# Rows 256 to 511 of x by two crossbar copies of 128 rows, with the early gate in 128-column halves, in a SwiGLU feed-forward kernel

## The chip, the cores and the metric

The kernel runs on one core of a Trainium2 chip. The metric is the device time of one execution in microseconds (us); the time before is the median of 3 runs. The engines named below are PE (TensorE, matrix multiplication; its weight loads are listed as PEld), ScalarE (ACT), VectorE (DVE), GpSimd (POOL) and SP, which here only issues transfers (DMA). A transfer that ScalarE issues stands in a queue of its own. Matmuls write to PSUM, which has few banks; everything else lives in SBUF, the on-chip memory of 128 partitions.

## The reference

```python
B, S, D, F = 1, 2048, 640, 1536          # x: B,S,D  w_gate, w_up: D,F  w_down: F,D, all bfloat16

def reference(x, w_gate, w_up, w_down):
    g = _silu(x @ w_gate)
    u = x @ w_up
    return (g * u) @ w_down
```

## The kernel before

**Tiles.** The 2048 rows of x are worked on in 4 blocks of 512 (`S_BLK`); D is 5 chunks of 128 (`KD`), F is 12 chunks of 128 (`KF`). The gate and up products are computed transposed: for each f chunk, PE multiplies a 128x128 piece of `wg_sb` (or `wu_sb`), loaded as weights, with 512 columns of `xT`, the transposed x, and adds up 5 such products in a PSUM tile `pg` (or `pu`) of 128 x 512. That is `proj` (L195 to L203), and its arguments `c0` and `c1` choose the columns of the block. `gate` (L210 to L217) follows: ScalarE writes silu(pg) to `sg` (L214), VectorE multiplies it with `pu` into `aT` (L215). When all 12 f chunks of a block are done, the down products (L273 and L302) give the block's output rows.

**How x gets transposed.** For the first block, rows 0 to 255 are loaded plainly into `x_sb` (L85, one load from SP's queue and one from ScalarE's), and PE transposes them (`transpose_chunk`, L183 to L193), with copies from PSUM by ScalarE and VectorE. Rows 256 to 511 come by a transposing crossbar copy straight from the HBM into `xT`: `turn_x(PE_X, SUB)` at L121, with `PE_X` = 2 and `SUB` = 4 in units of 128 rows; the copy itself is L109. The other blocks of x come by crossbar copies of 512 rows (L138, L322, L324).

**The order of the transfers.** SP issues in program order: one x load (L85); three loads of the first 512 columns of `w_gate`, kd by kd (L120; ScalarE's queue carries kd 2 and 3); the crossbar copy of rows 256 to 511 (L109); `wu_sb` for f chunks 0 and 1, then for 2 and 3 (L123, L124, issued at L82); the loads of `wg_sb` and `wu_sb` in two pieces of 4 chunks each (L126, L127); `wd_sb` (L128); the crossbar copy of the next 512 rows; `x_row` (L139), and transposing copies of w_gate (`wgT`, L134), which VectorE uses for the last 4 rows. Transfers take completion semaphores in turn from a set of eight, and from the ninth on each waits until the transfer eight places before it has landed.

**The head.** `head` (L219 to L254) sets the order of the first block by hand. PE does 18 warm-up matmuls on a tile of ones (L179), transposes two chunks of x (L188), and then works on the first 4 f chunks (`N_EARLY`): first on columns 0 to 255, kd by kd as the weights land (L240), the very first kd in two halves of 128 columns; then on columns 256 to 511 for each f chunk (L247 and L248, the matmuls being at L197), for which the crossbar copy is needed; then for each f chunk the up product over all 512 columns (L251), followed by `gate`. `keep_order` holds PE, ScalarE, VectorE and SP to the order in which the program states their instructions. The loop over the remaining f chunks (L257 to L267) follows. Its `pg` and `pu` tiles come from the same four PSUM buffers (tag `gu`) as the four early `pg`; the early `pu` use the buffers of the output tiles (`po_a`, `po_b`).

Of the kernel before, what the change touches and what calls it, by code (L numbers as in the profile page):

```python
# [10 lines left out]
def _body(  # L11
# [9 lines left out]
    P = nc.NUM_PARTITIONS  # L21
# [13 lines left out]
    S_BLK = 512  # L35
    NSB = S // S_BLK
    SUB = S_BLK // P
    DA = 512
    Q = 32
    N_WARM, N_EARLY = 18, 4  # L40
    T = 4
    WT_STEP = 4
    PE_X = 2
# [14 lines left out]
    wg_sb = consts.tile([P, KD, F], bf16)  # L58
# [19 lines left out]
    def wslice(a, b):  # L78
        return slice(a * P, b * P)
# [17 lines left out]
    def keep_order(engine):  # L97

        traced = [i for i in nc.cur_bb.bb.instructions if i.engine == engine]
        for a, b in zip(traced, traced[1:]):  # L100
            issue_order(a, b)
# [5 lines left out]
    def turn_x(c0, c1):  # L107
        s_sl = slice(c0 * P, c1 * P)
        nc.sync.dma_start_transpose(out=xT[:, :, s_sl], in_=xt_v[s_sl])  # L109
# [4 lines left out]
    for eng, k0, k1 in (  # L114
# [3 lines left out]
        (nc.sync, 4, 5),  # L118
    ):
        eng.dma_start(out=wg_sb[:, k0:k1, f_sl], in_=wg_v[:, k0:k1, f_sl])  # L120
    turn_x(PE_X, SUB)  # L121
    nc.scalar.activation(silu_first[:], ones[:, 0:1], ACT.Silu)
    load_w(nc.sync, wu_sb, wu_v, 0, N_EARLY // 2)  # L123
    load_w(nc.sync, wu_sb, wu_v, N_EARLY // 2, N_EARLY)  # L124
# [52 lines left out]
    def warm(n):  # L177
        for _ in range(n):
            nc.tensor.matmul(  # L179
                pw[:, 0:P], lhsT=ones[:], rhs=ones[:], start=True, stop=True  # L180
            )

    def transpose_chunk(c, parts):  # L183
        c_sl = slice(c * P, (c + 1) * P)
        for copy, tag, k0, k1 in parts:
            pt = psum.tile([P, k1 - k0, P], bf16, tag=tag, name="pt")
            for kd in range(k0, k1):
                nc.tensor.transpose(  # L188
                    out=pt[:, kd - k0, :],
                    in_=x_sb[:, c, kd * P : (kd + 1) * P],  # L190
                    identity=ident[:],
                )
            copy(out=xT[:, k0:k1, c_sl], in_=pt[:])  # L193

    def proj(ps, w_sb, fc, sb, c0, c1):  # L195
        for kd in range(KD):
            nc.tensor.matmul(  # L197
                ps[:, c0:c1],
                lhsT=w_sb[:, kd, fc * P : (fc + 1) * P],
                rhs=xT[:, kd, sb * S_BLK + c0 : sb * S_BLK + c1],  # L200
                start=(kd == 0),
                stop=(kd == KD - 1),
            )  # L203

    def gu_tiles():
        pg = psum.tile([P, S_BLK], f32, tag="gu", name="pg", bufs=4)
        pu = psum.tile([P, S_BLK], f32, tag="gu", name="pu", bufs=4)
        return pg, pu

    def gate(pg, pu, sb, fc, n_s):  # L210

        s0 = sb * S_BLK
        sg = work.tile([P, S_BLK], f32, name="sg")
        nc.scalar.activation(sg[:, 0:n_s], pg[:, 0:n_s], ACT.Silu)  # L214
        nc.vector.tensor_tensor(  # L215
            out=aT[:, fc, s0 : s0 + n_s], in0=sg[:, 0:n_s], in1=pu[:, 0:n_s], op=ALU.mult
        )  # L217

    def head():  # L219

        dve, act = nc.vector.tensor_copy, nc.scalar.copy
        split = [(act, "po_a", 0, 2), (dve, "po_b", 2, KD)]
        late = PE_X * P
        warm(N_WARM)
        transpose_chunk(0, split)
        transpose_chunk(1, split)  # L230
        pg = [
            psum.tile([P, S_BLK], f32, tag="gu", name="pg", bufs=4)
            for _ in range(N_EARLY)
        ]
        early = [(0, 0, P), (0, P, late)] + [(kd, 0, late) for kd in range(1, KD)]
        for kd, c0, c1 in early:
            for fc in range(N_EARLY):


                nc.tensor.matmul(  # L240
                    pg[fc][:, c0:c1],
                    lhsT=wg_sb[:, kd, wslice(fc, fc + 1)],
                    rhs=xT[:, kd, c0:c1],
                    start=(kd == 0 and c0 == 0),
                    stop=(kd == KD - 1),
                )
        for fc in range(N_EARLY):  # L247
            proj(pg[fc], wg_sb, fc, 0, late, S_BLK)  # L248
        for fc in range(N_EARLY):
            pu = psum.tile([P, S_BLK], f32, tag="po_b" if fc % 2 else "po_a", name="pu")  # L250
            proj(pu, wu_sb, fc, 0, 0, S_BLK)  # L251
            gate(pg[fc], pu, 0, fc, S_BLK)
        keep_order(mybir.EngineType.PE)
        keep_order(mybir.EngineType.Activation)  # L254

    head()
    for sb in range(NSB):  # L257
        n_s = S_BLK if sb < NSB - 1 else S_BLK - T
        for fc in range(KF):
            if sb == 0 and fc < N_EARLY:  # L260
                continue
            pg, pu = gu_tiles()
# [134 lines left out]
def kernel(tc, *args):  # L397
    _body(tc, *args)
    tc.close()
    tc.compile()  # L400
    _trim(tc.nc)
# [30 lines left out]
```

## Time and profile before

| what | value |
|---|---|
| median of 3 runs | 163.23 us (162.78 to 163.5) |
| the profiled execution, its own time | 163.16 us |
| its span, first to last instruction | 161.8 us |
| PE busy | 158.9 us (98%), 796 matmuls |
| weight loads (PEld) busy | 77.1 us (48%) |
| VectorE busy | 110.9 us (69%) |
| ScalarE busy | 42.7 us (26%) |
| chain that ended last | PE 96%, DMA 2%, SP's queue 1% |
| the 20 early gate matmuls on columns 256 to 511 | 272 ns each from start to end, 6.6 to 8.8 us |
| moved by transfers | 15.86 MB, 98 GB/s over the span |

The span lies inside the execution's own time; the difference, 1.36 us, is around it. A matmul's duration goes from its start to the modelled end of its result and so overlaps the next one; the distance from start to start is what counts for a row of them. The chain that ended last is found by going back from the last instruction, at each step to what released it or to the instruction before it on its engine.

### The profile page before, as it was taken

To read this page: it belongs to the slowest core of one execution; us is meant where nothing else is said; L and a number is where in the kernel's file an instruction comes from. 1 tells how busy PE (TensorE), PEld (TensorE's weight loads), DVE (VectorE), ACT (ScalarE), POOL (GpSimd) and SP (SyncE) were. 2 spreads that over 40 slices of the span, in tenths; PEclk is the share of its full clock that TensorE was granted. 3 is DMA by queue.
4 is the path that set the end of the run, shared out by engine and by line. 5 is a ranking of instruction groups with operands and counts; after the bars stand their busy time and mean duration, and the time that the engine had idled before them with its cause. 6 is when DMAs were issued, how large, how long until landed. Compare 5 with 4: busy or idle time off the path is not lost.

```text
span 161.8 us, 2113 instructions
## 1 busy us (share of the span) xinstructions
PE 158.9 (98%) x796; PEld 77.1 (48%) x796; DVE 110.9 (69%) x249; ACT 42.7 (26%) x74; POOL 0.6 (0%) x6
## 2 busy tenths in 40 slices
PE   8999999999999999999999999999999999999995
PEld 7754444444444444444444444444444444445454
DVE  1035223599469999989919999979964999993000
ACT  5131222112222222211222322221214222222121
POOL 1000000000000000000000000000000000000000
DMA  7999999995189991003110000000321000000312
GB/s 226 265 344 350 363 218 231 245 189 101 35 186 166 228 226 39 4 0 34 65 65 0 0 4 2 0 0 4 61 67 34 0 0 0 0 0 4 50 39 73
DMA packets 41801, 15.86 MB, mean 98 GB/s; under 512 B 33216, under 2 KB 41664, under 8 KB 41792
## 3 DMA queue, kind: packets, MB, share of 16 engines
q1 hardware_dynamic: 33296, 14.78, 38.0%
q10 hardware_dynamic: 8496, 0.95, 3.9%
q8 instruction: 6, 0.10, 0.3%
q14 instruction: 3, 0.02, 0.1%
HBM read 6.88 MB, written 2.62 MB: 59 GB/s over the span
## 4 chain that ended last, share of the span: by engine, by line
PE 96%; DMA 2%; SPq 1%; DVE 0%; issue 0%
PE pu L197 32%; PE pg L197 31%; PE po_a L302 26%; PE po_t L273 6%; DMA wg_sb<-in_w_gate_dram 2%; PE pg L240 1%; SPq L120 0%; SPq L85 0%; DVE ot_b L314 0%
## 5 line engine op out<-in xcount | busy, mean ns | idle before, releaser
L197 PE MATMUL pu<-xT,wu_sb 128*128 128x512 bf16 (+1 forms) x240 | 59.0, 379 | 0.0
L197 PE MATMUL pg<-xT,wg_sb 128*128 128x512 bf16 (+2 forms) x240 | 56.9, 370 | 0.0
L215 DVE TENSOR_TENSOR aT<-sg,pu 128x512 bf16<-128x512 f32 (+1 forms) x48 | 32.8, 683 | 32.3 <-PE pu L197 32.3
L214 ACT ACTIVATE sg<-pg 128x512 f32<-128x512 f32 (+1 forms) x48 | 28.5, 596 | 70.7 <-PE pg L197 65.7
L302 PE MATMUL po_a<-wd_sb,aT 128*128 128x512 bf16 (+2 forms) x216 | 42.8, 358 | 0.0
L150 DVE SCALAR_TENSOR_TENSOR prod<-wgT,x_row 128x640 f32<-128x640 bf16 x48 | 39.4, 821 | 1.1
L150 DVE SCALAR_TENSOR_TENSOR prod<-wuT,x_row 128x640 f32<-128x640 bf16 x48 | 39.5, 822 | 1.0
L197 PEld LDWEIGHTS <-wu_sb 128*128 128x128 bf16 x240 | 23.5, 98 | 28.0
L197 PEld LDWEIGHTS <-wg_sb 128*128 128x128 bf16 x240 | 23.5, 98 | 26.1
L302 PEld LDWEIGHTS <-aT 128*128 128x128 bf16 x216 | 20.7, 98 | 21.7
L311 ACT CAST ot<-po_a 128x512 bf16<-128x512 f32 (+1 forms) x17 | 9.5, 560 | 32.0 <-PE po_a L302 20.9
L273 PE MATMUL po_t<-aT,wd_sb 128*128 128x512 bf16 (+1 forms) x48 | 10.4, 366 | 0.0
L273 PEld LDWEIGHTS <-wd_sb 128*128 128x128 bf16 x48 | 4.7, 98 | 5.1
L314 DVE CAST ot_b<-po_a 128x128 bf16<-128x128 f32 x1 | 0.3, 292 | 9.9 <-PE po_a L302 9.9
L282 ACT CAST ot_t<-po_t 128x512 bf16<-128x512 f32 (+1 forms) x4 | 2.2, 558 | 11.6 <-PE po_t L273 11.6
L150 DVE DVE_READ_ACCUMULATOR prod<-wuT,x_row 128x1 f32 x48 | 4.0, 83 | 0.0
L150 DVE DVE_READ_ACCUMULATOR prod<-wgT,x_row 128x1 f32 x48 | 4.0, 82 | 0.0
L284 DVE STREAM_TRANSPOSE ot_q<-ot_t 128x512 bf16<-128x512 bf16 (+1 forms) x4 | 2.7, 678 | 1.7 <-ACT ot_t L282 1.7
L240 PE MATMUL pg<-xT,wg_sb 128*128 128x256 bf16 (+1 forms) x24 | 2.6, 255 | 0.4 <-DMA wg_sb<-in_w_gate_dram 0.4
L193 DVE COPY xT<-pt 128x384 bf16<-128x384 bf16 x2 | 0.7, 358 | 3.2 <-PE pt L188 3.1
L179 PE MATMUL pw<-ones 128*128 128x128 bf16 x18 | 2.1, 313 | 0.4 <-DVE ones L105 0.4
L240 PEld LDWEIGHTS <-wg_sb 128*128 128x128 bf16 x24 | 1.9, 98 | 0.8 <-DMA wg_sb<-in_w_gate_dram 0.7
(15 smaller groups left out, 7.7 us busy)
## 6 DMA issues: line engine op xcount, KB each, us to landing
wd_sb<-in_w_down_dram SPq DMA_DIRECT2D x1, 1920.0 KB, 13.6
out_dram<-ot SPq DMA_DIRECT2D x15, 128.0 KB, 1.7
wg_sb<-in_w_gate_dram SPq DMA_DIRECT2D x2, 640.0 KB, 8.0
wu_sb<-in_w_up_dram SPq DMA_DIRECT2D x2, 640.0 KB, 8.6
wu_sb<-in_w_up_dram SPq DMA_DIRECT2D x2, 320.0 KB, 5.1
x_row<-in_x_dram SPq DMA_DIRECT2D x1, 640.0 KB, 5.0
wg_sb<-in_w_gate_dram SPq DMA_DIRECT2D x3, 128.0 KB, 3.8
out_dram<-ot_q ACTq DMA_DIRECT2D x12, 32.0 KB, 1.9
```

What stands on the lines that cost most here:

```text
L150: nc.vector.scalar_tensor_tensor(out=prod[:], in0=wT[:, fc, :], scalar=1.0, in1=x_row[:, t, :], op0=ALU.mult, op1=ALU.mult, accum_out=acc[ ...
L179: nc.tensor.matmul(pw[:, 0:P], lhsT=ones[:], rhs=ones[:], start=True, stop=True)
L193: copy(out=xT[:, k0:k1, c_sl], in_=pt[:])
L197: nc.tensor.matmul(ps[:, c0:c1], lhsT=w_sb[:, kd, fc * P : (fc + 1) * P], rhs=xT[:, kd, sb * S_BLK + c0 : sb * S_BLK + c1], start=(kd == 0 ...
L214: nc.scalar.activation(sg[:, 0:n_s], pg[:, 0:n_s], ACT.Silu)
L215: nc.vector.tensor_tensor(out=aT[:, fc, s0 : s0 + n_s], in0=sg[:, 0:n_s], in1=pu[:, 0:n_s], op=ALU.mult)
L240: nc.tensor.matmul(pg[fc][:, c0:c1], lhsT=wg_sb[:, kd, wslice(fc, fc + 1)], rhs=xT[:, kd, c0:c1], start=(kd == 0 and c0 == 0), stop=(kd == ...
L273: nc.tensor.matmul(po_t[:], lhsT=wd_sb[:, kf, DA:D], rhs=aT[:, kf, sb * S_BLK : sb * S_BLK + n_t], start=(kf == 0), stop=(kf == KF - 1),)
L282: nc.scalar.copy(ot_t[:], po_t[:])
L284: nc.vector.transpose(out=ot_q[:], in_=ot_t[:])
L302: nc.tensor.matmul(po[:], lhsT=aT[:, kf, s0 : s0 + P], rhs=wd_sb[:, kf, c0:c1], start=(kf == 0), stop=(kf == KF - 1),)
L311: nc.scalar.copy(ot[:], po[:])
```

## The change

The crossbar copy of rows 256 to 511 is issued as two copies of 128 rows, one behind the other on SP. The gate products of the four early f chunks on these rows run in two passes: first columns 256 to 383 for f chunks 0 to 3, then columns 384 to 511 for f chunks 0 to 3. Each pass has 4 x 5 = 20 matmuls of 128 columns, each with its weight load, so that there are 40 in place of 20 of 256 columns. PE's first matmul of the first pass waits for the first copy, its first of the second pass for the second copy. All lines behind the change stand one or two lines lower in the changed kernel; the order of all other instructions on each engine stays the same. The extra transfer shifts the eight semaphores that transfers use in turn by one place.

```diff
@@ -118,7 +118,8 @@
         (nc.sync, 4, 5),
     ):
         eng.dma_start(out=wg_sb[:, k0:k1, f_sl], in_=wg_v[:, k0:k1, f_sl])
-    turn_x(PE_X, SUB)
+    turn_x(PE_X, PE_X + 1)
+    turn_x(PE_X + 1, SUB)
     nc.scalar.activation(silu_first[:], ones[:, 0:1], ACT.Silu)
     load_w(nc.sync, wu_sb, wu_v, 0, N_EARLY // 2)
     load_w(nc.sync, wu_sb, wu_v, N_EARLY // 2, N_EARLY)
@@ -244,8 +245,9 @@
                     start=(kd == 0 and c0 == 0),
                     stop=(kd == KD - 1),
                 )
-        for fc in range(N_EARLY):
-            proj(pg[fc], wg_sb, fc, 0, late, S_BLK)
+        for c0 in range(late, S_BLK, P):
+            for fc in range(N_EARLY):
+                proj(pg[fc], wg_sb, fc, 0, c0, c0 + P)
         for fc in range(N_EARLY):
             pu = psum.tile([P, S_BLK], f32, tag="po_b" if fc % 2 else "po_a", name="pu")
             proj(pu, wu_sb, fc, 0, 0, S_BLK)
```

## The prediction

> **What bounds the kernel now.** I read the chain of waits first: 96% of the span is TensorE (PE), and after one wait for a weight load no other piece comes from anything but PE until the closing eviction.
>
> ```profile
> 0.91 3.89 DMA wg_sb<-in_w_gate_dram
> 4.85 1.92 PE pg L240 x16
> 6.77 2.18 PE pg L197 x20
> 8.95 4.32 PE pu L197 x20
> ```
>
> The columns are start, length, what. The chain starts running without holes at 4.85 us, when the second piece of the gate weights has landed. The PE timeline of the first microseconds says the same, with the idle time and its releaser in brackets:
>
> ```profile
> 3.84 0.64 PE L240 MATMUL pg<-xT,wg_sb 128*128 128x128 bf16 x8
> 4.85 1.92 PE L240 MATMUL pg<-xT,wg_sb 128*128 128x256 bf16 x16 [0.37 <-DMA wg_sb<-in_w_gate_dram]
> 6.61 2.35 PE L197 MATMUL pg<-xT,wg_sb 128*128 128x256 bf16 x20
> 8.79 4.48 PE L197 MATMUL pu<-xT,wu_sb 128*128 128x512 bf16 x20
> 13.11 1.24 PE L197 MATMUL pg<-xT,wg_sb 128*128 128x512 bf16 x5
> ```
>
> The third row is the work that the change cuts up. It has no bracket: PE does not wait for the crossbar copy. How near that is comes from SP's timeline (issue start, issue length) and from the DMA view (last number: us from issue to landing, asked for one issue at a time).
>
> ```profile
> 1.86 1.64 SPq L109 DMA_TRANSPOSE xT<-in_x_dram  x1
> 3.55 1.33 SPq L82 DMA_DIRECT2D wu_sb<-in_w_up_dram  x2
> ...
> 44.56 2.83 SPq L109 DMA_TRANSPOSE xT<-in_x_dram  x1
> ```
>
> ```profile
> xT<-in_x_dram SPq DMA_TRANSPOSE x1, 4.6
> ...
> wu_sb<-in_w_up_dram SPq DMA_DIRECT2D x1, 320.0 KB, 4.8
> ```
>
> The copy lands at 1.86 + 4.6 = 6.46, PE reaches it at 6.61: 0.15 us of slack. The first wu load lands at 3.55 + 4.8 = 8.35; PE loads weights from it at 8.68: 0.33 of slack. The second lands near 4.25 + 5.4 = 9.65 (the pair's median is 5.1, so the other took 5.4) for 8.79 + 10 x 0.216 = 10.95: 1.3. The next wg load (issued 4.93, 6.5 to landing) lands at 11.43 for about 12.9: 1.5; the wu load after it (5.50 + 7.8 = 13.30) is needed at 13.97: 0.67. The tightest loads are thus the copy and the first wu load.
>
> **Part 1, the matmuls.** Removed: 20 matmuls of 256 columns (4 f chunks x 5 kd), 8.79 - 6.61 = 2.18 us, 109 ns each. Added: 40 of 128 columns, with 20 weight loads more. Price of one from two rows of that width, by form:
>
> ```profile
> L302 PE MATMUL po_a<-wd_sb,aT 128*128 128x128 bf16 x12 | 0.8, 219 | 0.0
> L240 PE MATMUL pg<-xT,wg_sb 128*128 128x128 bf16 x8 | 0.6, 220 | 0.0
> ```
>
> Each busy time is (count - 1) spacings plus one duration. At the kernel's end: (0.8 - 0.219)/11 = 0.053 us. At L240, with the timeline's 0.64: (0.64 - 0.220)/7 = 0.060. Both have a new weight load for every matmul, as the new code has. I take 0.0555, between them: 40 x 0.0555 = 2.22, so +0.04; ends -0.06 and +0.22. The far bound is the 18 warm-up matmuls of the same width, (2.10 - 0.313)/17 = 0.105 us apart, which would make +2.0; they run before 2.5 us with durations of 313 ns, and the L240 row, 3 us before the place in question, has 220, so I leave that end to a rival.
>
> The Trainium skill, in "TensorE: Matmul & The Clock Gate", section "Back-to-back issue gap", speaks against the edit: in a stream of weight load and matmul pairs it gives about 81 ns for each of 128 columns, against 56 for one alone. By it the part would be an estimated 40 x 0.081 - 2.18 = +1.1 us, and the time some 164.2. The two rows above show the smaller figure, but in runs of 8 and 12, not 40, and the measured spacing decides for me.
>
> **Part 2, who waits for the gate.** The gate of chunk 0 is complete after 25 of the 40, at 6.61 + 25 x 0.0555 = 8.0 instead of about 7.2, the others 0.28 apart. ScalarE's silus start near 8.2 in place of 7.35 and run 0.6 each, so three are done by 10.0. Their reader is VectorE's product, which waits for pu: 10.14, 11.22, 12.30, 13.38 in the timeline. The fourth silu waits for the first product today (10.87) and still will. Nothing of it reaches PE, whose next use of a gate buffer is at 13.11. Cost 0, cover 1.3 us and more.
>
> **Part 3, the copies' issue on SP.** A copy of 256 rows takes 1.64 us to issue, one of 512 rows 2.83. That is 0.45 fixed and 0.60 per 128 rows; one of 128 takes about 1.05, two 2.1, and everything behind them on SP (all wu, wg and wd loads, the next crossbar copies) is issued 0.45 later. From the ninth transfer on, each DMA of the queue waits for the one eight before it, and the extra copy turns this by one: the first wu load now waits for the x load that lands at 0.12 + 2.9 = 3.0 (SP is there after 3.9), the next wg load for ScalarE's wg load that lands at 0.55 + 4.1 = 4.65 (SP is there at about 5.4). Neither binds. The 0.45 is covered too: the first wu load is issued at 3.55, but the rings still carry the crossbar packets until about 6.05, a cover of 2.5 us. Without that cover the load would land at 8.80 and cost 0.1.
>
> **Part 4, the copies on the rings.** The DMA columns of the table by stretches (the last two: share, GB/s) show what a crossbar copy does there:
>
> ```profile
> 4.50:4.75 0.25, 0.00 (x0) 0.00 (x0) 0.00 (x0) 0.00 (x0) 0.00 (x0) 1.00 1.69 176
> 4.75:5.00 0.25, 0.15 (x2) 0.14 (x3) 0.00 (x0) 0.00 (x0) 0.00 (x0) 1.00 0.36 80
> 5.00:5.25 0.25, 0.25 (x4) 0.23 (x3) 0.00 (x0) 0.00 (x0) 0.00 (x0) 1.00 1.29 287
> ...
> 6.00:6.25 0.25, 0.25 (x5) 0.23 (x3) 0.00 (x0) 0.00 (x0) 0.00 (x0) 1.00 1.09 150
> ...
> 48.75:49.00 0.25, 0.25 (x3) 0.13 (x2) 0.25 (x1) 0.08 (x1) 0.00 (x0) 1.00 0.30 71
> 49.00:49.25 0.25, 0.25 (x3) 0.13 (x2) 0.25 (x1) 0.25 (x1) 0.00 (x0) 1.00 0.43 102
> ```
>
> The bytes and the 256 B packets stay the same; what a second copy can add is a second start. The start at 4.5 to 5.0 loses, against 290 GB/s, (114 + 210) x 0.25 = 81 KB, 0.28 us. Between two crossbar copies behind each other, 48.5 to 50.25, the same count (190, 71, 102, 158, 182, 130, 223 GB/s) loses 243 KB, 0.84 us; but those are limited by their issue of about 3 us for 655 KB, and here the second copy is issued by about 4.0, before the first has run. So the gap is between 0 (loss goes with the rows, not the copies: 0.84 for 512 rows is 0.42 for 256, about what the front copy loses) and 0.84; I take 0.28. Then the first half lands by 6.46 at the latest, for 6.61; the second at 6.74, and PE gets to it after 20 matmuls, 6.61 + 1.11 = 7.72: hidden by 1.0. The first wu load lands at 8.63, wanted at 8.68 + 0.04: hidden by 0.1. With 0.84 it lands at 9.19 and PE stalls 0.47; the later loads have more slack than that, so the stall isn't paid twice.
>
> **The sum.** The profiled execution took 163.16 us, 161.8 of span and 1.36 around it; the median of the three runs is 163.23. Matmuls +0.04, the rest 0: 163.20 on the profiled time, 163.27 on the median. I predict 163.3. What the split opens, gate work before all 256 rows are there, buys nothing, since PE has other work until 6.61 and the copy is there at 6.46.
>
> **The rivals.**
> *A start for each copy.* The gap is 0.84, the first wu load stalls PE at 8.7: 163.2 + 0.47 = 163.7. For it: the low stretch after each crossbar copy around 48 and 55 us. Against: issue limits those.
> *The copies run one after the other.* The second starts only when the first has landed: 0.4 from last byte (6.05) to landing (6.46), and about 1.1 from issue to first byte (the x load issued at 0.00 shows no byte before 1.0), a gap of 1.5. Both the second half (7.96 for 7.72) and the first wu load (9.85 for 8.72) are late; the latter decides, 1.1 us of stall: 164.3, slower. It counts as slower from a gap of 1.2 on. For it: the bandwidth falls almost to nothing between copies at times. Against: no wait stands between them in the program.
> *Forty small matmuls don't hold the spacing.* At the warm-up's 0.105: 165.2, slower. Against it: 8 and 12 in a row hold 0.06 and less, and the granted clock is 1.00 throughout.
> *A gain.* The split does nothing for the gate, but a smaller first copy pushes fewer crossbar packets (from 4.0 us on) beside the last wg pieces, and PE's wait before 4.85 (0.37 idle, about 0.5 between starts) goes: 162.7. Against it: the copies still start at the same place in the queue.
>
> **How the numbers follow.** Less than 0.5%, 0.8 us, can't be told from no change: runs of the same kernel lie between 162.78 and 163.5. Forecast 0.48, all of it same. A start for each 0.14 (0.09 same, 0.05 slower). One after the other 0.17, slower. Spacing 0.08, slower. A gain 0.13 (0.05 same, 0.08 faster, since the runs' spread of 0.4 lies on top). Together: faster 0.08, same 0.62, slower 0.30. The likeliest alone gives 162.9 to 163.7. The range reaches down to the gain, 162.6, and up to the copies one after the other, 164.3.
>
> **What would show it.** Right: 40 matmuls of 128 columns in L198 from 6.6 to about 8.85, no bracket on the first pu row, two crossbar issues of about 1 us, the chain still PE from 4.85 on. Wrong: an idle entry of PE on xT near 7.7 or on wu_sb near 8.8, as long as the gap; a spacing well over 0.06 in the 40; or a first L240 row of 256 columns that starts elsewhere than at 4.85.

## The result, and the profile after

The changed kernel takes 163.82 us (median of 22 runs, 163.14 to 164.47), the kernel before 163.19 (22 runs, 162.74 to 163.85). The ratio is 1.0034, with a 95% interval of 1.0019 to 1.0048: slower by about a third of a per cent, 0.55 us, inside the bound of 0.5% that the prediction calls no change. Executions more than 1.5% above the fastest of their kernel are left out of this ratio and of those below. The profiled execution has a span of 162.2 us (own time 163.58) against 161.8 (163.16). It is one of the shorter ones: 6 of the 22 lie between 164.09 and 164.47, none of the kernel before's does, and no profile of the changed kernel is of such an execution. The other 16 have a median of 163.65.

In PE's timeline of the changed kernel (start, length, what; in brackets idle time and releaser) the split itself is nearly free, and a wait stands where there was none:

```profile
6.50 2.40 PE L198 MATMUL pg<-xT,wg_sb 128*128 128x128 bf16 x40
...
13.05 1.24 PE L198 MATMUL pg<-xT,wg_sb 128*128 128x512 bf16 x5
14.52 1.25 PE L198 MATMUL pu<-xT,wu_sb 128*128 128x512 bf16 x5 [0.23 <-DMA wu_sb<-in_w_up_dram]
```

The 40 small matmuls start at 6.50 and the next row at 8.73: 2.23 us where the 20 wide ones took 2.18. The five gate matmuls of f chunk 4 start at 13.05, so the up product would follow at 13.05 + 1.08 = 14.13; it starts at 14.52, 0.39 us late. (The bracket counts from the modelled end of the last matmul and so shows only 0.23.) The account of the profiled span: PE reaches the gate 0.11 us earlier (6.50 for 6.61), the matmuls +0.05, the wait +0.39, together +0.33; the last eviction starts at 160.28 instead of 159.93, +0.35.

The chain of waits, over the first 15 us, no longer runs through PE there, but back through that load to SP's issues:

```profile
1.86 1.27 SPq L109
...
3.18 1.27 SPq L109
...
4.50 0.58 SPq L82
...
5.13 0.53 SPq L82
...
5.70 0.52 SPq L82
...
6.27 8.21 DMA wu_sb<-in_w_up_dram
...
14.52 0.60 PE pu L198 x2
```

Two crossbar issues of 1.27 us stand in place of one of 1.64, so the first wu load is issued at 4.50 instead of 3.55 (0.95 later) and the wu load of f chunks 4 to 7 at 6.27 instead of 5.50 (0.77 later). The latter lands at 14.47 (6.27 + 8.2) instead of 13.30. What the later issue does on the rings shows in the stretches of 0.25 us (last two columns: DMA share, GB/s):

```profile
5.25:5.50 0.25, 0.25 (x4) 0.23 (x3) 0.00 (x0) 0.00 (x0) 0.00 (x0) 1.00 0.99 197
5.50:5.75 0.25, 0.25 (x5) 0.22 (x4) 0.00 (x0) 0.00 (x0) 0.00 (x0) 1.00 0.21 41
5.75:6.00 0.25, 0.25 (x5) 0.23 (x3) 0.00 (x0) 0.00 (x0) 0.00 (x0) 1.00 0.51 116
6.00:6.25 0.25, 0.25 (x5) 0.23 (x3) 0.00 (x0) 0.00 (x0) 0.00 (x0) 1.00 1.07 153
```

Nearly all crossbar packets are through by 5.5, and the wu packets, issued a microsecond later than before, are not there yet. The kernel before moved about 290 GB/s from 5.0 to 6.0:

```profile
5.25:5.50 0.25, 0.25 (x4) 0.23 (x3) 0.00 (x0) 0.00 (x0) 0.00 (x0) 1.00 1.28 291
5.50:5.75 0.25, 0.25 (x5) 0.22 (x4) 0.00 (x0) 0.00 (x0) 0.00 (x0) 1.00 1.22 289
5.75:6.00 0.25, 0.25 (x5) 0.23 (x3) 0.00 (x0) 0.00 (x0) 0.00 (x0) 1.00 1.23 291
```

### The profile page after: what moved, and what is told of

It is laid out like the page before. It is cut to its first block, busy times and chain, and to the rows that moved or that the text cites. A ratio compares the mean times of both kernels' runs of the same rounds, so it can differ in the third digit from the quotient of the medians.

```text
span 162.2 us, 2154 instructions
## 1 busy us (share of the span) xinstructions
PE 159.6 (98%) x816; PEld 77.8 (48%) x816; DVE 110.9 (68%) x249; ACT 42.7 (26%) x74; POOL 0.6 (0%) x6
## 4 chain that ended last, share of the span: by engine, by line
PE 90%; DMA 5%; SPq 4%; issue 0%; DVE 0%
PE pu L198 29%; PE pg L198 29%; PE po_a L304 26%; PE po_t L275 6%; DMA wu_sb<-in_w_up_dram 5%; SPq L109 2%; SPq L82 1%; SPq L120 1%; SPq L85 0%; DVE ot_b L316 0%
## 5 line engine op out<-in xcount | busy, mean ns | idle before, releaser
L198 PEld LDWEIGHTS <-wg_sb 128*128 128x128 bf16 x260 | 23.8, 98 | 25.9
L284 ACT CAST ot_t<-po_t 128x512 bf16<-128x512 f32 (+1 forms) x4 | 2.2, 559 | 11.6 <-PE po_t L275 11.6
L241 PE MATMUL pg<-xT,wg_sb 128*128 128x256 bf16 (+1 forms) x24 | 3.2, 303 | 0.0
L241 PEld LDWEIGHTS <-wg_sb 128*128 128x128 bf16 x24 | 2.5, 122 | 0.5 <-DMA wg_sb<-in_w_gate_dram 0.2
```

The source lines that it names most:

```text
L198: nc.tensor.matmul(ps[:, c0:c1], lhsT=w_sb[:, kd, fc * P : (fc + 1) * P], rhs=xT[:, kd, sb * S_BLK + c0 : sb * S_BLK + c1], start=(kd == 0 ...
L241: nc.tensor.matmul(pg[fc][:, c0:c1], lhsT=wg_sb[:, kd, wslice(fc, fc + 1)], rhs=xT[:, kd, c0:c1], start=(kd == 0 and c0 == 0), stop=(kd == ...
L284: nc.scalar.copy(ot_t[:], po_t[:])
```

## The experiments

Twelve kernels ran (one of them the changed kernel again), each several times in turn with the kernel before on the same chip; ratios are to those runs of it, with a 95% interval in brackets. "Landing" is issue start plus us to landing in the DMA view.

### The halves alone and the copies alone

The changed kernel with `turn_x(PE_X, SUB)` put back, and the kernel before with the two `turn_x` calls:

```diff
-    turn_x(PE_X, PE_X + 1)
-    turn_x(PE_X + 1, SUB)
+    turn_x(PE_X, SUB)
```

> One crossbar copy of 256 rows as before, the early gate in 40 matmuls of 128 columns as after. Issue theory (the two copies take SP 2.60 us to issue in place of 1.64, so all loads behind them are issued 0.95 later, the rings run dry and the wu load of f chunks 4 to 7 lands 0.39 too late): no stall here, span 161.8 to 161.9, ratio 1.000. Ring theory (a second crossbar copy costs a second start on the rings, whenever it is issued): the same, 1.000. Matmul theory (40 small matmuls cost more than 20 wide ones): the loss of the change stays, ratio 1.003; by the spacing of 0.0555 us it would be +0.04 us.

Measured: 1.0007 (0.9991 to 1.0023), span 161.8, no stall.

```profile
6.50 2.39 PE L197 MATMUL pg<-xT,wg_sb 128*128 128x128 bf16 x40
8.73 4.48 PE L197 MATMUL pu<-xT,wu_sb 128*128 128x512 bf16 x19
```

Forty in a row again take 8.73 - 6.50 = 2.23 us, 0.056 apart. The small matmuls are thus not the price by themselves.

> Two crossbar copies of 128 rows as after, the early gate in 20 matmuls of 256 columns as before. Issue theory and ring theory: a stall of PE of about 0.4 us on the wu load of f chunks 4 to 7 as in the changed kernel, ratio 1.002 to 1.004. Matmul theory: no stall, ratio 1.000.

Measured: 1.0038, but with a wide interval, 1.0013 to 1.0064: the medians are 163.54 and 163.35, and 4 of its 12 runs lie above 164.1. Its profiled execution is one of these (span 164.0):

```profile
4.30 4.45 PE L241 MATMUL pg<-xT,wg_sb 128*128 128x128 bf16 x24 [0.46 <-DMA wg_sb<-in_w_gate_dram]
```

These 24 matmuls take 2.8 to 3.4 us in most other profiles, so PE is 2 us late from the start and waits for nothing later. The ratio lies in the range that was expected, but it doesn't support the theory: it comes from those 4 executions. The other 8 lie between 163.37 and 163.56, about 0.15 us above the kernel before, and in the profile the wu load of f chunks 4 to 7 lands at 13.57, not near 14.4.

### The issue alone, without a second copy

The kernel before with two small loads into a tile `spare` that nothing reads:

```diff
     turn_x(PE_X, SUB)
+    for n in range(2):
+        nc.sync.dma_start(out=spare[:, n, :], in_=x2[0:P, n * 16 : (n + 1) * 16])
```

> The kernel before with two loads of 128 x 16 elements (4 KB each) into a spare tile put on SP behind the one crossbar copy; nothing reads them. They keep SP some 0.85 us and move next to no bytes. Issue theory: the first wu load is issued near 4.4 in place of 3.55, the rings run dry behind the crossbar packets, the wu load of f chunks 4 to 7 lands about 14.4 and PE stalls 0.3 to 0.4, ratio 1.002 to 1.003. Ring theory: no second crossbar start, so it lands by 13.7 at the latest, no stall, ratio 1.000.

SP's timeline of this kernel:

```profile
1.86 1.59 SPq L110 DMA_TRANSPOSE xT<-in_x_dram  x1
3.50 1.05 SPq L124 DMA_DIRECT2D spare<-in_x_dram  x2
4.60 1.00 SPq L83 DMA_DIRECT2D wu_sb<-in_w_up_dram  x2
```

Measured: 1.0010 (1.0001 to 1.0020). The first wu load is issued at 4.60, as late as in the changed kernel, and the rings run dry as there (85 GB/s from 6.0 to 6.5, against 202 before). But the wu load of f chunks 4 to 7 lands at 13.31, on time; the lateness shows further back (the next two weight loads land 0.5 and 0.6 us later than before, the first third of the transposed w_gate at 31.95 instead of 30.90). Late issue alone is thus not the loss; the expectation of 14.4 was wrong.

### The two waits, and their remedies

Smaller pieces in the changed kernel, so that the piece of wu that PE wants first comes earlier:

```diff
-    W_CHUNKS = [(4, 8), (8, 12)]
+    W_CHUNKS = [(4, 6), (6, 8), (8, 12)]
```

> The changed kernel with the loads of wg and wu for f chunks 4 to 7 cut into two pieces of two chunks each (wg 4-5, wu 4-5, wg 6-7, wu 6-7), so that the piece of wu that PE wants at 14.1 stands 320 KB earlier in the queue. If the stall on that load is the whole loss (issue theory and ring theory alike): no wait of PE on wu_sb, ratio 1.000 to 1.001. If the time went elsewhere (matmul theory): 1.003 as in the changed kernel.

Measured: 1.0026 (1.0004 to 1.0048), against the expectation. PE's wait on wu_sb is gone, but the chain of waits shows another in block 0, through the transposed w_gate that VectorE reads:

```profile
24.71 7.95 DMA wgT<-in_w_gate_dram
...
34.49 0.83 DVE prod L151 x2
35.32 0.64 DVE ot_q L286
...
38.02 0.59 ACT ot L313
...
38.66 3.40 PE po_a L304 x15
```

That copy lands near 32.6. VectorE's three dot products, then the output transpose, ScalarE's four issues and its copy of the first output tile follow each other, and PE's third output tile waits for the copy: block 0's down products take 10.78 us instead of 10.52, 0.26 lost. In the kernel before the copy lands at 30.90 and the same ScalarE copy ends at 37.13, over a microsecond before PE wants the buffer.

So I formed a second theory: SP's whole stream is late, and it is a matter of the execution and of the remedy at which wait it surfaces. Four kernels followed: the changed kernel again, with the dot products moved behind the transpose, with less issue on SP, and the move in the kernel before as a control.

> The changed kernel, unaltered, for a second profile beside the next three. If its loss comes from the one late wu load of f chunks 4 to 7: the same stall near 14.1, ratio 1.003. Late-stream theory (all transfers of SP's queue are late by about 1 us from the second copy on; which wait that becomes depends on the execution: the wu load of f chunks 4 to 7, whose slack was 0.67, or the first third of the transposed w_gate, which was 1.3 us ahead of the point from which VectorE's dot products hold up the output transpose, ScalarE's issues and copies, and so PE's third output tile at 38.3): ratio 1.003 as well, with the transposed w_gate landing at 32.0 to 32.6 in place of 30.9.

Measured: 1.0043 (1.0017 to 1.0068), and the same wait:

```profile
8.77 4.48 PE L198 MATMUL pu<-xT,wu_sb 128*128 128x512 bf16 x19
...
14.71 1.25 PE L198 MATMUL pu<-xT,wu_sb 128*128 128x512 bf16 x5 [0.38 <-DMA wu_sb<-in_w_up_dram]
```

Without it the second row would start 5.40 us behind the first (25 matmuls of 512 columns), at 14.17: 0.54 lost. Of its 12 executions 5 lie above 164.3; the profiled one (163.73) is again one of the others.

The dot products moved, in the changed kernel:

```diff
-        do_dots(3)
+        if sb > 0:
+            do_dots(3)
         nc.vector.transpose(out=ot_q[:], in_=ot_t[:])
...
-                if 0 < j and not last:
+                if (0 < j or sb == 0) and not last:
                     do_dots(3)
```

> The changed kernel with the three dot products that stand ahead of the output transpose in block 0 moved behind it (VectorE does them after the first output tile instead; their number up to the end of the block stays the same). Late-stream theory: the late transposed w_gate can no longer hold up PE, so what is left is the stall on the wu load where it happens: ratio down to 1.000 to 1.002. If the loss is only the wu load, or the start of the kernel: 1.003 as in the changed kernel.

Measured: 1.0032 (1.0016 to 1.0048). The transposed w_gate is 1.9 us later than before (32.81) and holds up nobody, but the wait on the wu load is there, from 14.31 to 14.91.

> The kernel before with the same move of three dot products as in the run above: a control of what the move does by itself. Late-stream theory: in the kernel before the transposed w_gate is 1.3 us early, so nothing changes, ratio 0.999 to 1.000.

Measured: 0.9995 (0.9980 to 1.0011), as expected: the move does nothing by itself.

> The changed kernel with both moves at once: wg and wu for f chunks 4 to 7 in pieces of two chunks, and the three dot products of block 0 behind the output transpose. Late-stream theory (each move alone left PE one of two waits: the small pieces a wait behind the transposed w_gate of 0.26 us, the later dots a wait of 0.44 us on the wu load): neither wait in the profile, ratio 1.000 to 1.0015. If the loss lies somewhere else (the start, the 40 matmuls): 1.003 still.

The edits are those of the small pieces and of the later dots. Measured: 0.9997 (0.9980 to 1.0013). The whole loss is gone, with the two copies and the 40 matmuls still in place, and none of the 12 executions lies above 163.62.

```profile
8.90 4.48 PE L198 MATMUL pu<-xT,wu_sb 128*128 128x512 bf16 x20
...
30.48 2.75 PE L275 MATMUL po_t<-aT,wd_sb 128*128 128x512 bf16 x12
```

From the first up product to the first down product it is 30.48 - 8.90 = 21.58 us, as in the kernel before (30.37 - 8.79), where the changed kernel has 30.72 - 8.73 = 21.99. The matmuls and the crossbar copies themselves are thus cleared; what cost was two loads that came too late. It doesn't beat the kernel before. The rows of the first down product, in the kernel before and in the changed kernel:

```profile
30.37 2.75 PE L273 MATMUL po_t<-aT,wd_sb 128*128 128x512 bf16 x12
```

```profile
30.72 2.75 PE L275 MATMUL po_t<-aT,wd_sb 128*128 128x512 bf16 x12
```

### Three edits of the issue

Less issue on SP: the wg load of kd 4 becomes part of ScalarE's:

```diff
-        (nc.scalar, 2, 4),
+        (nc.scalar, 2, 5),
         (nc.sync, 1, 2),
-        (nc.sync, 4, 5),
```

> The changed kernel with the load of wg for kd 4 taken from SP (0.47 us of issue) and made part of ScalarE's load of kd 2 and 3, so that the two crossbar copies are issued from 1.39 instead of 1.86 and everything behind them 0.47 earlier. Issue as the cause of the late stream: the first wu load is issued near 4.03 in place of 4.50, the wu load of f chunks 4 to 7 and the transposed w_gate land about 0.45 sooner, ratio 1.000 to 1.0015. Ring theory: the second copy's own start stays, the stream is as late as in the changed kernel, ratio 1.003. A risk for both: kd 4 lands later than 6.1, where PE wants it.

Inconclusive: 1.0020 (1.0000 to 1.0039). Its profiled execution took 166.09, 2.4 us above the median: the wg load of kd 1 landed at 5.51 instead of 4.81, PE waited 0.90 for it, and the 16 gate matmuls behind took 3.59 us in place of 1.92. Whether ScalarE's larger load made that load late is not shown.

The two early wu loads from ScalarE's queue:

```diff
-    load_w(nc.sync, wu_sb, wu_v, 0, N_EARLY // 2)
-    load_w(nc.sync, wu_sb, wu_v, N_EARLY // 2, N_EARLY)
...
         transpose_chunk(1, split)
+        load_w(nc.scalar, wu_sb, wu_v, 0, N_EARLY // 2)
+        load_w(nc.scalar, wu_sb, wu_v, N_EARLY // 2, N_EARLY)
```

> The changed kernel with the two early wu loads issued from ScalarE's queue (behind its two copies of the transposed x, near 3.8) instead of SP's, so that the crossbar copies hold up nothing but the wg and wu loads behind them, which now come 1.15 us sooner than in the changed kernel. Issue theory: the rings don't run dry behind the crossbar packets, the wu load of f chunks 4 to 7 lands by 13.5, no wait of PE on it, ratio 0.999 to 1.001. Ring theory: the second copy's own start stays, ratio 1.002 to 1.003. A risk for both: packets of two queues share the rings, so the second crossbar copy or the last wg pieces may land later.

Measured: 1.0123 (1.0087 to 1.0159). The risk that was named came about:

```profile
6.73 1.28 PE L196 MATMUL pg<-xT,wg_sb 128*128 128x128 bf16 x20
8.89 1.28 PE L196 MATMUL pg<-xT,wg_sb 128*128 128x128 bf16 x20 [0.88 <-DMA xT<-in_x_dram]
```

The second crossbar copy lands at 8.88 instead of 6.58, and PE stands before the second half. That the wu packets of the other queue held it up is likely, but not shown. The run tells nothing about the issue, but shows what the second half's slack was worth.

Four copies of 64 rows in the kernel before:

```diff
-    turn_x(PE_X, SUB)
+    for c in range(4):
+        s_sl = slice(PE_X * P + c * 64, PE_X * P + (c + 1) * 64)
+        nc.sync.dma_start_transpose(out=xT[:, :, s_sl], in_=xt_v[s_sl])
```

> The kernel before (20 matmuls of 256 columns) with rows 256 to 511 in four crossbar copies of 64 rows. Issue theory: a copy costs SP about 0.9 us whatever its size and 0.35 per 128 rows (1.60 for 256, 1.27 for 128), so four take 4.3 to 4.5 with the gaps; the first wu load is issued near 6.4 in place of 3.55, the rings stand empty from about 6 on, that load lands near 10.2 and PE waits for it about 1.4 us from 8.8 on: ratio 1.007 to 1.011. If the issue went with the rows (0.35 per 64 rows): issued at 3.6 as before, ratio 1.000. Ring theory with 0.28 us lost per further start: 0.5 us over the slack of the tightest load, 1.003 to 1.005.

Measured: 1.0199 (1.0170 to 1.0227), median 166.59. SP's timeline:

```profile
1.86 5.14 SPq L123 DMA_TRANSPOSE xT<-in_x_dram  x4
7.05 1.15 SPq L82 DMA_DIRECT2D wu_sb<-in_w_up_dram  x2
```

Each issue takes 1.25 us, as much as one of 128 rows (1.27). So the issue has a floor here: cutting a copy from 256 rows (1.64) to 128 saves SP 0.37 per copy, and below 128 next to nothing. The loss is about twice what was expected. The profiled execution took 169.15, 2.6 us above the median, so its parts are not those of the median: PE waits 1.61 for the last copy, 0.57 for the wg load and 1.72 for the wu load of f chunks 4 to 7, and after that the next ten matmuls of 512 columns take 3.7 us in place of 2.2. The expectation had one wait alone, on the first wu load.

### Both causes together, without a second copy

One thing didn't fit: with equally late issue the wu load of f chunks 4 to 7 landed at 13.31 in one kernel and at 14.65 in another. The transfers of the instruction queue are the likely cause. There is one between 9 and 16 us in the profiles of the table below; in the DMA view of a stretch of 0.5 us (queue, count, MB, share of 16 engines) it is this line, from 13.5 us on in the kernel before, and from 11.5 on in the changed kernel's second profile:

```profile
q8 instruction: 1, 0.02, 14.6%
```

It is one packet and takes 0.146 x 16 x 0.5 = 1.17 us, on one of the 16 rings. In the traces the completion count of each load goes up 16 times, and the load has landed at the last step. The table has the step before it too:

| kernel | gate matmuls | fetch at | wg of chunks 4-7 lands | wu: 15 of 16 steps by | wu lands | PE waits for it |
|---|---|---|---|---|---|---|
| before | 20 wide | 13.6 | 11.43 | 12.73 | 13.30 | no |
| dots later (control) | 20 wide | 13.0 | 11.67 | 13.16 | 13.54 | no |
| issue alone | 20 wide | 13.5 | 11.44 | 13.03 | 13.31 | no |
| copies alone | 20 wide | 14.9 | 11.70 | 13.42 | 13.57 | no |
| halves alone | 40 | 11.6 | 10.93 | 12.82 | 13.90 | no |
| changed | 40 | 12.1 | 12.50 | 14.22 | 14.47 | 0.39 |
| changed, again | 40 | 11.9 | 11.70 | 13.59 | 14.65 | 0.54 |
| changed, dots later | 40 | 11.5 | 11.90 | 13.66 | 14.86 | 0.60 |

With 40 more PE instructions (20 matmuls, 20 weight loads) the fetch comes 1 to 2 us sooner in these profiles. In three of the four profiles with an early fetch (11.5 to 11.9) the last step lags the other 15 by 1.1 to 1.2 us, about the length of the fetch, and the load lands 3.0 us behind the wg load; in those with a late one it lags by 0.2 to 0.6, and the landings lie 1.9 apart. That the ring that lags is the one with the fetch is inferred from this, not seen. The first profile of the changed kernel is an exception: no single ring lags, six steps come after 13.7, the wg load itself is late, with a rate of 221 GB/s from 8.5 to 9.0 us, and the cause of that is open. Other profiles have other fetch times, which the number of PE instructions alone doesn't explain: 10.2 and 10.5 with the small pieces and with both remedies; 13.2, 14.6 and 16.1 with the wu loads on ScalarE's queue, with less issue on SP and with four copies, where PE runs late. The last run put the two causes together without a second crossbar copy (the edit of the issue alone, on the kernel with the halves alone).

> One crossbar copy of 256 rows as before, but with the early gate in 40 matmuls of 128 columns and the two small spare loads on SP behind the copy (the edits of the runs with the halves alone and the issue alone together; nothing reads the spare loads). Each alone gave next to nothing, 1.0007 and 1.001. Theory of two causes meeting (the issue makes SP's stream about 0.5 us late, and the 40 extra PE instructions bring the instruction fetch, one transfer of 1.2 us on one of the 16 rings, from 13.0 to 13.6 forward to 10.2 to 12.1, in front of the end of the wu load of f chunks 4 to 7, which then lands about 1 us later): the fetch at 11.4 to 12.1, that load at 14.3 to 14.7, PE waits on it 0.2 to 0.6, ratio 1.002 to 1.004 with no second crossbar copy. Ring theory (the second crossbar copy is what costs): the load by 13.7, no wait, ratio 1.000 to 1.0015.

Measured: 1.0033 (1.0021 to 1.0046), the ratio of the changed kernel itself. The fetch is at 12.0 and the wu load lands at 14.31, 3.27 behind the wg load, as expected; 15 of its 16 steps are done by 12.85. The wait that was expected isn't in this profile:

```profile
9.05 4.48 PE L200 MATMUL pu<-xT,wu_sb 128*128 128x512 bf16 x20
...
30.64 2.75 PE L277 MATMUL po_t<-aT,wd_sb 128*128 128x512 bf16 x12
```

It is 21.59 us from row to row, so nothing is lost between. PE is 0.26 us behind the kernel before already at the first row (its 16 gate matmuls of 256 columns took 2.36 us, there 1.92), and wants the load at 9.05 + 5.40 = 14.45. At the pace of the kernel before it would want it at 14.19, and wait some 0.15. The late landing without a second copy is thus shown; that the wait makes up the whole ratio, 0.54 us, is not.

## Why the prediction was right, and where its sum was not

The verdict and the range held: 163.3 forecast, 163.82 measured, no change by the 0.5% bound. The sum did not: +0.04 us stood there, +0.55 was measured. That the verdict held is in part luck, as the loss that the sum missed happens to stay below the bound of 0.8 us. Of the prediction's signs, the 40 matmuls and the pu row without a bracket came true; the issues of about 1 us and the chain on PE from 4.85 on did not. By its steps:

- **What bounds the kernel:** right. PE sets the pace from the first wg landing on, but for the one wait of 0.39 us, and there is no gain from gate work that could start earlier: the first half landed at 5.56, PE came at 6.50.
- **Part 1, the matmuls:** right: 0.0555 taken, (2.40 - 0.219)/39 = 0.0559 measured, +0.05 for +0.04. The 81 ns of the Trainium skill ("TensorE: Matmul & The Clock Gate", section "Back-to-back issue gap") is not what 40 pairs in a row show here; the measured 56 ns decides.
- **Part 2, the silus:** right: they start at 8.09 (8.2 forecast) and end long before their readers.
- **Part 3, the issue:** the mis-sized term. 0.45 us fixed and 0.60 per 128 rows came from 256 and 512 rows and was drawn through to 128: 1.05. Measured: 1.27, and 1.25 for 64 rows. The first wu load was issued 0.95 us later and the next two loads 0.77, not 0.45. The cover of the rings by the crossbar packets gave out: they fell to 41 GB/s from 5.50 to 5.75. The turned waits of the eight semaphores didn't bind, as forecast: SP's issues follow each other without holes.
- **Part 4, the rings:** the landings of the next two loads were right (the second copy 6.58 for 6.74, the first wu load 8.40 for 8.63) and hidden as said. Wrong was the sentence "the later loads have more slack than that, so the stall isn't paid twice". The price was computed for the tightest load at the head of the queue, but a delay of the stream reaches all that follows. The wu load of f chunks 4 to 7 had 0.67 us (0.8 to the start of its matmuls), landed 1.2 to 1.6 later in the three profiles of the table that wait, and decided. The transposed w_gate, which was not looked at, comes next: with the small pieces it was what held PE.
- **Not in the prediction at all:** the instruction fetch, which comes earlier in the profiles with 40 more PE instructions, and the landing of one load about 1 us later with it. Halves alone and late issue alone cost 0.07% and 0.10% by their ratios (at most 0.23% and 0.20% by their intervals); together, even without a second copy, 0.33% (0.21% to 0.46%). That the two make more together than their sum, 0.17%, is likely, but not clear of the intervals.
- **The rivals:** *a start for each copy* came near in size (163.7) by another mechanism and at another load. *One after the other* did not happen: the second copy landed 1.0 us behind the first, with its issue. *Spacing* fell. So did *a gain*: the gate's rows come 0.11 us earlier, but as much with the halves alone, which have the one copy.

What stays open: why some executions are longer, 6 of 22 and 5 of 12 of the changed kernel and 4 of 12 of the copies alone above 164.05 us, against none of 22 and of 35 and 3 of 35 of the kernel before beside them (the one profile of them, of the copies alone, shows a slow start of PE; whether two copies make that more frequent was not tried); the rate of 221 GB/s in the changed kernel's first profile; and that the fetch follows the number of instructions and delays the load is read off the profiles of the table, not tried by moving the fetch alone.

## What to carry to other kernels

Cutting a transfer in two costs its queue a second issue, and with a floor under the issue the parts cost almost as much as the whole. List the slack of every load behind it in the queue, not only of the next one, as far as a reader that holds up the main engine by detours. Extra instructions on a saturated engine can cost nothing where they run and still, as the profiles here suggest, move a fetch that shares the transfer rings.

## What the runs showed of the hardware that was not expected

- A crossbar copy holds SP's sequencer 1.25 us for 64 rows of 640, 1.27 for 128, 1.5 to 1.6 for 256 and 2.3 to 3.7 for 512. The 512-row copy that is issued right behind the stream of weight loads holds it far longer, 11.95 us before and 11.32 after, so the rows alone don't set the time.
- One instruction fetch is a single packet of 0.88 to 1.18 us on one ring. In four profiles (halves alone, changed again, changed with the dots later, and the last run) a load that was on its way had one of its 16 completion steps 1.1 to 1.5 us behind the others.
- PE starts at half speed for a time that differs between executions. The 8 matmuls of 128 columns at the start of the gate took 0.62 us in some profiles and 1.06 in others (0.057 and 0.107 apart); in the profile of the copies alone the half speed lasted to about 8.8 us and the span was 164.0. The granted clock in the table of stretches reads 1.00 all the while, so the spacing has to be looked at. (In the profile of the four copies, half speed after the wait of 1.72 us does show there, as 0.50 from 19 to 21 us.) The Trainium skill ("TensorE: Matmul & The Clock Gate", section "What's actually happening") ascribes such a start to a clock gate with a window that runs free of the kernel, and lets its end vary by about 500 ns. The lengths here, from about 3.4 us to about 8.8, vary far more, and no run tested why.
